# First attention batch in tiles of 6, 6, 6 and 5 steps, its first tile scattered in two parts, and the last values moved around the last second mix

## The chip, the cores and the metric

The kernel runs on one core of one Trainium2 chip. The metric is device time in microseconds (us) of a whole execution; the kernel before has a median of 1279.26 us over three runs. Five engines appear below: PE (TensorE: matmuls into PSUM), DVE (VectorE), ACT (ScalarE), POOL (GpSimd) and SP (SyncE, which here only issues transfers). Transfers issued by SP or ACT run on the core's 16 DMA engines.

## What is computed

Attention with two mixes over the heads (4 batches, 12 heads, 448 rows, 64 columns), then two feed-forward layers over the 1792 tokens:

```python
scores = scale * np.matmul(q, k.transpose(0, 1, 3, 2))
scores = np.einsum('bhij,hg->bgij', scores, w_pre)       # first mix, over heads
scores = scores - np.max(scores, axis=-1, keepdims=True)
attn = np.exp(scores)
attn = attn / (np.sum(attn, axis=-1, keepdims=True) + 1e-09)
attn = np.einsum('bhij,hg->bgij', attn, w_post)          # second mix, over heads
x = np.matmul(attn, v)                                   # (B, H, S, D) -> x (B*S, H*D)
...
gate = 1.0 / (1.0 + np.exp(-(x @ w_gate)))
x = gate * (x @ w_val) @ w_out                           # 768 -> 1536 -> 768
h = np.maximum(x @ w_in, 0.0)
return (h * h @ w_out2).astype(np.float32)               # 768 -> 2048 -> 768
```

## The kernel before

**Tiles and steps.** The rows of a batch are cut into tiles, and a tile into steps of 20 rows (`STEP`). A batch has 23 steps: 92 steps in all. `row_tiles` (L34) gives tiles of 6, 6, 6, 5 steps, but for batch 0 tiles of 3, 5, 5, 5, 5. So there are 17 tiles; tile 0 is steps 0 to 2, tile 1 steps 3 to 7, and batch 1 begins with step 23, batch 2 with step 46, batch 3 with step 69. The last tile of a batch has one step with half of its rows.

**What a tile needs.** `scores` (L192) makes the product of q and k for one tile and one of the 6 pairs of heads (eight matmul records), copies it from PSUM into a buffer `e` (rows on partitions), and scatters `e` with two transfers, one for each head, into `g`, where heads and rows lie on partitions as the first mix needs them. There are two `g`, used by even and odd tiles in turn, and six buffers `e`. A tile thus costs 12 scatters (210 KB each with 120 rows). The scores of a tile are spread over the first steps of the tile before (`plan`, L336 to 346). In the very beginning ("early", L376 to 383) the six pairs of tile 0 and four pairs of tile 1 are made first; there the two heads' PSUM banks are copied by ACT and by DVE, and of most pairs the second head's scatter is issued by ACT.

**What a step needs.** `premix` (L220, matmul line L226) is the first mix from `g`; DVE takes the maximum (L242), ACT the exponential (L250), DVE the reciprocal of the sum (L258, L259), POOL the scaled weights `wn` (L262), PE the second mix (`postmix`, L278), and DVE copies its PSUM into the buffer of mixed rows `ap` (`mixed`, L294). Step s issues the second mix of step s-3, the first mix of step s, and the scores or values planned for s, each engine strictly in the written order.

**Values.** When a tile's mixed rows are complete, `values` (L296, matmul line L313) multiplies them with v: three calls for each tile, 40 matmul records each, followed by DVE copies (L331). They are planned 3, 4 and 5 steps into the next tile. For the last tile but one they stand at steps 91, 92 and 93, for the last tile at 94, where also the last second mix (of step 91) is issued.

**SP.** One list of transfers in fixed order: q of a tile (`q_load`), k and v of a batch (224 KB and 320 KB for a pair of heads), the scatters, and for the feed-forward part `raw` (weights from HBM, 384 KB), `gv` (converted weights back to HBM, three of 384 KB and one of 192 KB for each conversion) and `w`. Once `sp.open` is set, a scatter waits until the sixth transfer before it in the list has landed, any other until the third before it (`Window`, L514).

**The feed-forward part** is placed by a planner (`Feed`): each step of attention gives it some modelled time, in which it hands out conversions and operand work to idle places of DVE, ACT, POOL and SP. From the end of the values on, PE does 4290 matmuls (L953) back to back.

Of the kernel before, what the change touches and what calls it, by code (L numbers as in the profile page):

```python
# [9 lines left out]
F32 = mybir.dt.float32  # L10
# [10 lines left out]
GI = 10  # L21
STEP = 2 * GI
HB = GI // 2
# [10 lines left out]
def row_tiles(b, S):  # L34

    n = -(-S // STEP)
    lengths = [n // 4 + (t < n % 4) for t in range(4)]
    if b == 0:
        lengths = [3] + [(n - 3) // 4 + (t < (n - 3) % 4) for t in range(4)]
    cuts = [0]  # L40
    for x in lengths:
        cuts.append(min(cuts[-1] + x * STEP, S))
    return list(zip(cuts, cuts[1:], lengths))
# [4 lines left out]
    return (length * STEP - (i1 - i0)) // GI * GI  # L48


def row_order(i0, i1, length):

    c, lead = length * GI, skipped(i0, i1, length)
    rows = []
    for y in range(2):
        for r in range(HB):
            for g in range(2 * length):  # L60
                rows.append(min(max(y * c + g * HB + r - lead, 0), i1 - i0 - 1) + i0)
    return rows


def attention(tc, feed, q, k, v, w_pre, w_post, B, H, S, D):
# [10 lines left out]
    nc = tc.nc  # L76
    sp = feed.sp
    NP = H // 2
    JB = S // HP
# [5 lines left out]
    tiles, steps, starts = [], [], []  # L85
    for b in range(B):
        for i0, i1, length in row_tiles(b, S):
            lead = skipped(i0, i1, length)
# [4 lines left out]
    NT, NS = len(tiles), len(steps)  # L93
    starts.append(NS)
    sizes = [t[3] * STEP for t in tiles]
    IM = max(sizes)
# [7 lines left out]
    with ExitStack() as ctx, ExitStack() as mix, ExitStack() as low, ExitStack() as top, ExitStack() as left:  # L104
# [17 lines left out]
        wr = p0.tile([P, 2, H], F32, name="wr")  # L122
        mask = p0.tile([P, HB, H], F32, name="mask")
        first = ap[1][:HP, :HB, :H]
        g_of = [None, None]
        for m, x in zip(((NT - 1) % 2, NT % 2), pg):
            g_of[m] = x.tile([P, GT, S], F32, name=f"g{m}")
# [63 lines left out]

        def scores(n, p, ps, early=None):  # L192

            b, _, _, length, _ = tiles[n]
            isz = sizes[n]
            kt = k_t.pop((b, p)) if last_of(n) else k_t[b, p]
            for c in range(0, isz, HP):
                c1 = min(c + HP, isz)
                for o in range(2):
                    r = slice(o * D, (o + 1) * D)  # L200
                    nc.tensor.matmul(  # L201
                        ps[c:c1, o, :S] if early is None else ps[o][c:c1, :S], lhsT=q_t[n][r, p, c:c1], rhs=kt[r], start=True, stop=True
                    )
            e = p4.tile([IM, 2, S], F32, tag="e", name="e")
            if early is None:
                nc.scalar.copy(e[:isz], ps[:isz, :, :S])  # L206
            else:
                nc.scalar.copy(e[:isz, 0], ps[0][:isz, :S])
                nc.vector.tensor_copy(e[:isz, 1], ps[1][:isz, :S])
            to = g_of[n % 2][G0 : G0 + GI * H].rearrange("(r h) g j -> h r g j", h=H)  # L210
            for o in range(2):
                x = dict(out=to[2 * p + o, :, : 2 * length], in_=e[:isz, o])
                if o and early:
                    nc.scalar.dma_start(**x)
                else:
                    sp.dma_start(**x, depth=2 * DEPTH)

        a_t = {}

        def premix(s):  # L220
            n, t, ys = steps[s]
# [69 lines left out]

        def mixed(n, t, ps):
            to = mixed_of(n)[:, :, t * GI : (t + 1) * GI].rearrange("p x (u i) -> p u x i", i=HB)
            nc.vector.tensor_copy(to, ps[:, :, : JB * KH].rearrange("p u (x i) -> p u x i", i=HB))  # L294

        def values(n, i):  # L296

# [49 lines left out]
        for n in range(NT):  # L347
            s0 = starts[n + 1] + LAG
            if n + 1 < NT:
                at = [s0, s0 + 1, s0 + 2]  # L350
                if n + 2 == NT:
                    at = [NS - 1, NS, NS + 1]
            else:
                at = [s0 - 1] * 3
            for i in range(NP // VP):
                plan[at[i]].append(("values", n, i))

        loads = {s: [] for s in range(NS + 12)}
        for i in range(NP):
            loads[i // 2].append((v_load, 0, i))  # L360
        firsts = [n for n in range(1, NT) if tiles[n][0] != tiles[n - 1][0]]
        for n in firsts:
            b = tiles[n][0]
# [8 lines left out]
            k_load(0, p)  # L372
            k_load(0, p + 1)
        masks()
        q_load(1)
        early = [(0, p) for p in range(NP)] + [(1, p) for p in range(fetched[1])]  # L376
        with tc.tile_pool(name="ps_s", bufs=1, space=PSUM, **kw) as ps_s:
            ps = [ps_s.tile([P, BANK], F32, name=f"ps_s{m}") for m in range(8)]
            for m, (n, p) in enumerate(early):
                x = 2 * m % 8  # L380
                scores(n, p, ps[x : x + 2], m % 4 != 3)
                if m == NP - 1:
                    mixers()
        ps_t = ctx.enter_context(tc.tile_pool(name="ps_t", bufs=1, space=PSUM, reuse_waits="tile", **kw))
        ps_m = mix.enter_context(tc.tile_pool(name="ps_m", bufs=1, space=PSUM, reuse_waits="tile", side="left"))
        pair_m = [ps_m.tile([P, 2, BANK], F32, name=f"ps_m{m}") for m in range(2)]
        pair_x, pair_y = (ps_t.tile([P, 2, BANK], F32, name=f"pair_{m}") for m in "xy")
        q_load(2)
        sp.open = True

        for s in range(NS + LAG):
# [46 lines left out]
            if 9 <= s < NS:  # L438
                n, t, _ = steps[s]
                if t < quiet[n]:  # L440
                    feed.free["SP"] = feed.now + 3.3
                feed.step(3.3)
            elif s >= NS:
                feed.step(3.0)


# [847 lines left out]
```

## Time and profile before

| what | before |
|---|---|
| median of 3 runs (lowest to highest) | 1279.26 us (1277.84 to 1281.04) |
| profiled execution | 1274.76 us, its span 1273.0 us |
| PE busy | 1221.9 us (96%) |
| PE weight loads busy | 1029.4 us (81%) |
| DVE busy | 909.2 us (71%) |
| ACT busy | 722.9 us (57%) |
| POOL busy | 300.0 us (24%) |
| chain that ended last, by engine | PE 89%, DVE 4%, DMA 3%, ACT 2%, issue 2% |

The span begins at the first instruction of the trace. Attention takes the first 383 us of it, the feed-forward layers the other 890 us. PE is the engine nearly everywhere, so what counts is where PE waits or runs at the lower of its two clocks.

### The profile page before, as it was taken

The page shows a single profiled execution, that of the slowest core. Times are in us where ns is not written, and L with a number is a line of the kernel's source. Part 1 is how long each engine was busy: PE and PEld are TensorE (multiplying, and loading weights), DVE is VectorE, ACT ScalarE, POOL GpSimd, SP SyncE. Part 2 cuts the span into 40 slices and gives each one's busy share as a digit, 9 for nine tenths or more (in the row PEclk, how much of TensorE's full clock was granted, in tenths as well). Part 3 has the DMA queues.
Part 4 walks back from the last instruction along what each step waited for, and adds up shares of the span by engine and source line. Part 5 has one row for each costly group of instructions (what it writes and reads, how often), then busy time and mean ns, then how long its engine had stood idle before and what let it go on. Part 6 is the DMA issues. An engine that isn't in the chain of part 4 may idle for free.

```text
span 1273.0 us, 31908 instructions
## 1 busy us (share of the span) xinstructions
PE 1221.9 (96%) x12882; PEld 1029.4 (81%) x12882; DVE 909.2 (71%) x1498; ACT 722.9 (57%) x1317; POOL 300.0 (24%) x381
## 2 busy tenths in 40 slices
PE   6999899989979999999999999999999999999998
PEld 2566566656658999899999999998889999999997
DVE  3667576757776567776657898577998788887621
ACT  4666667556645566576566538545566556336610
POOL 4223232314354323314232001123223220000000
PEclk9999999999979999999999999999999999999999
DMA  6666767675616987778996322757787875441231
GB/s 206 192 221 192 238 192 240 199 234 183 223 42 227 316 283 269 257 233 276 304 296 236 116 62 81 237 179 250 257 308 227 288 247 161 119 124 51 66 111 53
DMA packets 118927, 254.54 MB, mean 200 GB/s; under 512 B 12476, under 2 KB 65276, under 8 KB 118780
## 3 DMA queue, kind: packets, MB, share of 16 engines
q1 hardware_dynamic: 117840, 251.42, 60.6%
q8 instruction: 101, 1.65, 0.5%
q10 hardware_dynamic: 940, 1.09, 0.3%
q14 instruction: 46, 0.38, 0.1%
HBM read 153.71 MB, written 59.18 MB: 167 GB/s over the span
## 4 chain that ended last, share of the span: by engine, by line
PE 89%; DVE 4%; DMA 3%; ACT 2%; issue 2%; SPq 0%; POOL 0%; DVEq 0%; ACTq 0%; POOLq 0%
PE ps L953 67%; PE pair_y L313 6%; PE ps_m L226 5%; PE pair_x L278 4%; PE ps_m L201 3%; PE pair_y L201 2%; DMA g<-e 2%; DVE c L969 1%; ACT e L206 1%; DVE c L940 1%; ACT a L250 1%; PE ps_s L201 1%; DVE w L927 1%; DMA v<-in_v 0%; SPq L515 0%
## 5 line engine op out<-in xcount | busy, mean ns | idle before, releaser
L953 PE MATMUL ps<-c,w 128*128 128x448 f32 x4290 | 879.6, 367 | 6.4 <-ACT w L924 2.0
L953 PEld LDWEIGHTS ps<-c,w 128*128 128x128 f32 x4290 | 807.0, 188 | 78.8 <-ACT ps L977 2.5
L927 DVE TENSOR_TENSOR w<-w,w 128x768 fp32r<-128x768 f32 x189 | 198.7, 1052 | 149.4 <-ACT w L924 148.7
L829 POOL TENSOR_TENSOR y<-y,raw 128x384 int32<-128x384 int32 x136 | 157.7, 1182 | 470.3 <-DVE y L823 167.2
L924 ACT CAST w<-w 128x768 fp32r<-128x768 f32 x189 | 157.5, 835 | 161.0 <-PE ps L953 140.7
L937 ACT CAST c<-c 128x448 fp32r<-128x448 f32 x250 | 127.7, 565 | 70.0 <-DVE c L969 65.8
L940 DVE TENSOR_TENSOR c<-c 128x448 fp32r<-128x448 f32 x248 | 151.9, 661 | 9.6 <-ACT c L937 6.4
L969 DVE TENSOR_TENSOR c<-ps,c 128x448 f32<-128x448 f32 x172 | 105.7, 621 | 74.2 <-PE ps L953 68.5
L250 ACT ACTIVATE a<-ps_m,nm 128x448 f32<-128x448 f32 x180 | 112.8, 635 | 55.4 <-DVE nm L242 50.6
L262 POOL TENSOR_SCALAR wn<-wq,sm 128x60 f32<-128x60 f32 x180 | 75.5, 435 | 248.2 <-DVE sm L259 170.0
L242 DVE TENSOR_REDUCE nm<-ps_m 128x2 f32<-128x896 f32 (+1 forms) x92 | 98.2, 1069 | 47.0 <-PE ps_m L226 45.7
L278 PEld LDWEIGHTS pair_x<-wn,a 64*64 64x64 f32 x5040 | 91.7, 137 | 40.9 <-issue 21.5
L313 PEld LDWEIGHTS pair_y<-ap,v 128*64 128x64 f32 x2040 | 85.5, 142 | 34.9 <-issue 21.4
L294 DVE COPY ap<-pair_x 128x840 f32<-128x840 f32 x92 | 94.6, 1029 | 22.8 <-PE pair_x L278 21.5
L226 PE MATMUL ps_m<-g,wp 64*64 64x448 f32 (+1 forms) x720 | 91.3, 559 | 16.1 <-DMA g<-e 7.9
L278 PE MATMUL pair_x<-wn,a 64*64 64x60 f32 x5040 | 97.8, 222 | 8.4 <-POOL wn L262 5.9
L977 ACT COPY c<-ps 128x448 f32<-128x448 f32 x128 | 67.3, 533 | 62.8 <-PE ps L953 60.6
L313 PE MATMUL pair_y<-ap,v 128*64 128x60 f32 (+4 forms) x2040 | 96.5, 251 | 5.8 <-DVE ap L294 3.2
L969 DVE TENSOR_TENSOR c<-c 128x448 f32<-128x448 f32 x160 | 97.1, 641 | 1.8
L206 ACT COPY e<-ps_m 120x896 f32<-120x896 f32 (+1 forms) x46 | 41.6, 905 | 51.1 <-PE ps_m L201 50.5
L817 ACT ACTIVATE raw<-raw 128x768 f32<-128x768 f32 x68 | 62.3, 917 | 0.0
L820 ACT ACTIVATE raw<-raw 128x768 int32<-128x768 uint32 x68 | 62.3, 916 | 0.0
(49 smaller groups left out, 602.2 us busy)
## 6 DMA issues: line engine op xcount, KB each, us to landing
w<-gv SPq DMA_DIRECT2D x84, 384.0 KB
g<-e SPq DMA_DIRECT2D x108, 210.0 KB
raw<-in_wo SPq DMA_DIRECT2D x56, 384.0 KB
w<-wi SPq DMA_DIRECT2D x56, 384.0 KB
w<-wo SPq DMA_DIRECT2D x49, 384.0 KB
wo<-y SPq DMA_DIRECT2D x42, 384.0 KB
g<-e SPq DMA_DIRECT2D x81, 175.0 KB
gv<-y SPq DMA_DIRECT2D x36, 384.0 KB
```

The costliest lines, as they stand in the source:

```text
L226: nc.tensor.matmul(ps[u * HP : (u + 1) * HP, y, :S], lhsT=wp[r], rhs=g_of[n % 2][r, 2 * t + u], start=True, stop=True,)
L242: nc.vector.tensor_reduce(out=nm[:, ys], in_=a_t[s][0][:, ys, :S], op=ALU.max, axis=AX.X, negate=True)
L250: nc.scalar.activation(a[:, y], ps[:, y, :S], AF.Exp, bias=nm[:, y : y + 1], accum_out=sm[:, y : y + 1])
L278: nc.tensor.matmul(out[c : c + HP, u, 2 * k + (y if j < JB - 1 else 0)], lhsT=a[r, y, j * HP : (j + 1) * HP], rhs=wn[r, y].rearrange("p g ...
L313: nc.tensor.matmul(ps[o * D : (o + 1) * D, lo : lo + to], lhsT=w[:, o, j], rhs=rhs, start=j == 0, stop=j == JT - 2, skip_group_check=j >= ...
L829: e.tensor_tensor(out=y3, in0=y3, in1=of(raw.tile.bitcast(I32)[:, :, 0])[:, i], op=ALU.add)
L924: e.copy(dst.tile[:, 0], flat())
L927: e.tensor_tensor(out=dst.tile[:, 1], in0=flat(), in1=dst.tile[:, 0].bitcast(F32), op=ALU.subtract)
L937: e.copy(hi.tile, src.tile)
L940: e.tensor_tensor(out=lo.tile, in0=src.tile, in1=hi.tile.bitcast(F32), op=ALU.subtract)
L953: e.matmul(bank.tile, lhsT=a[k], rhs=x[l], start=start and n == 0, stop=stop and n == 2, skip_group_check=more,)
L969: e.tensor_tensor(out=out.tile, in0=a.tile, in1=b.tile, op=op)
```

## The change

- Batch 0 is cut like the others: tiles of 6, 6, 6, 5 steps; 16 tiles instead of 17, with the same 92 steps. Tile 0 is now steps 0 to 5, tile 1 steps 6 to 11.
- Tile 0's 120 rows are laid out so that partitions 0 to 59 of its score buffer hold what steps 0 to 2 need, and 60 to 119 what steps 3 to 5 need (`parts_of`, and `row_order` on the host). Its 12 scatters become 24 of half the size: first the first halves of all pairs, then, behind the last pair, the second halves of all pairs in reverse order, all of these on SP.
- Tile 0's score buffers are no longer the six `e` but pieces of the buffers of mixed rows (`spare`), five of `ap1` and one of `ap0`, which are not yet used then.
- In the beginning, q of tile 1 is loaded after the scatters of the second pair instead of ahead of all scatters; tile 1's scatters are all issued by SP; q of tile 2 and v of batch 0 are issued at steps 0 and 3 onwards instead of ahead of and at step 0 (in the list q of tile 3 stands ahead of q of tile 2).
- At the end, the values of the last tile but one move from steps 91, 92, 93 to 92, 93, 94, so that their third call stands behind the last second mix. The copy of that last second mix is split between DVE and ACT, and for the step before it the planner keeps DVE and ACT free of feed-forward work for 3 us of its modelled time.

```diff
     lengths = [n // 4 + (t < n % 4) for t in range(4)]
-    if b == 0:
-        lengths = [3] + [(n - 3) // 4 + (t < (n - 3) % 4) for t in range(4)]
...
+def parts_of(b, i0, length):
+
+    if b == 0 and i0 == 0:
+        return [(0, length), (length, 2 * length)]
+    return [(0, 2 * length)]
...
-    for y in range(2):
-        for r in range(HB):
-            for g in range(2 * length):
-                rows.append(min(max(y * c + g * HB + r - lead, 0), i1 - i0 - 1) + i0)
+    for g0, g1 in parts:
+        for y in range(2):
+            for r in range(HB):
+                for g in range(g0, g1):
+                    rows.append(min(max(y * c + g * HB + r - lead, 0), i1 - i0 - 1) + i0)
...
+        spare = []
+        for x in ap[::-1]:
+            x = x.rearrange("p x c -> p (x c)")[:, HB * (IM // 2) :]
+            x = x[:, : x.shape[1] // (2 * S) * 2 * S].rearrange("p (n o s) -> p n o s", o=2, s=S)
+            spare += [x[:, n] for n in range(x.shape[1])]
...
-            e = p4.tile([IM, 2, S], F32, tag="e", name="e")
+            if n == 0:
+                e = spare[p][:IM]
+            else:
+                e = p4.tile([IM, 2, S], F32, tag="e", name="e")
...
-            for o in range(2):
-                x = dict(out=to[2 * p + o, :, : 2 * length], in_=e[:isz, o])
-                if o and early:
-                    nc.scalar.dma_start(**x)
+            for m, (g0, g1) in enumerate(parts_of(b, i0, length)):
+
+                def scatter(m=m, g0=g0, g1=g1):
+                    for o in range(2):
+                        x = dict(out=to[2 * p + o, :, g0:g1], in_=e[g0 * GI : g1 * GI, o])
+                        if o and early and not m:
+                            nc.scalar.dma_start(**x)
+                        else:
+                            sp.dma_start(**x, depth=2 * DEPTH)
+
+                if m:
+                    late.append(scatter)
                 else:
-                    sp.dma_start(**x, depth=2 * DEPTH)
+                    scatter()
...
-            nc.vector.tensor_copy(to, ps[:, :, : JB * KH].rearrange("p u (x i) -> p u x i", i=HB))
+            x = ps[:, :, : JB * KH].rearrange("p u (x i) -> p u x i", i=HB)
+            if n == NT - 1 and t == tiles[n][3] - 1:
+                nc.vector.tensor_copy(to[:, 0], x[:, 0])
+                nc.scalar.copy(to[:, 1], x[:, 1])
+            else:
+                nc.vector.tensor_copy(to, x)
...
-                    at = [NS - 1, NS, NS + 1]
+                    at = [NS, NS + 1, NS + 2]
...
-            loads[i // 2].append((v_load, 0, i))
+            loads[3 + i // 2].append((v_load, 0, i))
...
-        q_load(1)
...
-                scores(n, p, ps[x : x + 2], m % 4 != 3)
+                scores(n, p, ps[x : x + 2], n == 0 and m != 3)
+                if m == 1:
+                    q_load(1)
                 if m == NP - 1:
                     mixers()
+                    for x in late[::-1]:
+                        x()
+        loads[0].append((q_load, 2))
...
-        q_load(2)
...
+                if s == NS + 1:
+                    for e in ("ACT", "DVE"):
+                        feed.free[e] = max(feed.free[e], feed.now + 3.0)
                 feed.step(3.0)
```

**SP in the beginning.** First what SP issues from its start up to step 3 or so in the kernel before, then in the changed one (`g_189` and `g_190` are the two `g`, `e` and `ap_...` the score buffers they are filled from):

```order
L515 DMA q<-in_q 128x600
L515 DMA g_189<-e 10x6x448 x7
L515 DMA g_190<-e 10x10x448 x5
L515 DMA q<-in_q 128x600
L515 DMA g_190<-e 10x10x448 x4
L515 DMA q<-in_q 128x600
L515 DMA v<-in_v 128x640 x6
```

```order
L548 DMA g_190<-ap_186 10x6x448 x2
L548 DMA q<-in_q 128x720
L548 DMA g_190<-ap_186 10x6x448 x4
L548 DMA g_190<-ap_185 10x6x448 x3
L548 DMA g_190<-ap_186 10x6x448 x10
L548 DMA g_189<-e 10x12x448 x12
L548 DMA q<-in_q 128x600
L548 DMA q<-in_q 128x720
L548 DMA v<-in_v 128x640 x6
```

Tile 0's scatters on SP grow from 7 to 19, tile 1's from 9 to 12, and the q that step 6's scores read now stands behind all of them.

**SP around the beginning of batch 2.** The scatters of the last tile of batch 1 (10 groups of 10 rows, `10x10x448`), then what stands between them and the scatters of the first tile of batch 2; before, then after:

```order
L515 DMA g_189<-e 10x10x448 x12
L515 DMA q<-in_q 128x720
L515 DMA k<-in_k 128x448 x3
L515 DMA raw<-in_wg 128x768
L515 DMA g_190<-e 10x12x448 x12
```

```order
L548 DMA g_189<-e 10x10x448 x12
L548 DMA q<-in_q 128x720
L548 DMA k<-in_k 128x448
L548 DMA raw<-in_wg 128x768 x2
L548 DMA k<-in_k 128x448
L548 DMA raw<-in_wg 128x768 x2
L548 DMA k<-in_k 128x448
L548 DMA gv_139<-y 128x384
L548 DMA g_190<-e 10x12x448 x12
```

Three loads of weights and one store have moved ahead of these scatters; in the kernel before, the same list (with `in_wv`) stands one batch later, ahead of the scatters of step 69.

**PE at the end of attention.** From the first mix of the last step on, second mixes (`pair_x`), values of the last tile but one (`64x120` and `64x60`) and the beginning of the last tile's values (`64x100`); before, then after:

```order
L226 MATMUL ps_m_327<-g_189,wp 64x448 x4
L313 MATMUL pair_y<-ap_186,v 64x120 x2
...
L278 MATMUL pair_x<-wn,a 64x60 x28
...
L278 MATMUL pair_x<-wn,a 64x60 x28
...
L313 MATMUL pair_y<-ap_186,v 64x120 x4
L278 MATMUL pair_x<-wn,a 64x60 x28
L313 MATMUL pair_y<-ap_185,v 64x100 x2
```

```order
L248 MATMUL ps_m_345<-g_189,wp 64x448 x4
L300 MATMUL pair_x<-wn,a 64x60 x28
...
L300 MATMUL pair_x<-wn,a 64x60 x28
...
L300 MATMUL pair_x<-wn,a 64x60 x28
L340 MATMUL pair_y<-ap_185,v 64x120 x2
...
L340 MATMUL pair_y<-ap_185,v 64x120 x4
L340 MATMUL pair_y<-ap_186,v 64x100 x2
```

The call of values that stood ahead of the first of these three second mixes now stands behind the last one, ahead of the last tile's values.

## Rows read from the trace of the kernel before

**Rows 1.** Windows: stretch, length, busy us (instructions) by engine, clock, DMA share, GB/s

```profile
18.59:41.33 22.74, 16.73 (x321) 8.04 (x321) 11.00 (x20) 12.63 (x28) 3.66 (x9) 0.85 0.72 231
41.33:106.01 64.68, 61.68 (x1649) 39.16 (x1649) 45.58 (x93) 42.04 (x93) 18.28 (x39) 1.00 0.62 198
106.01:359.27 253.26, 233.72 (x6137) 155.74 (x6140) 184.27 (x364) 158.35 (x353) 79.51 (x155) 0.98 0.65 207
359.27:382.88 23.61, 18.42 (x431) 15.63 (x422) 15.07 (x27) 10.17 (x21) 12.26 (x14) 0.78 0.19 53
382.88:1273.00 890.12, 879.65 (x4292) 807.00 (x4290) 646.60 (x983) 492.40 (x812) 174.95 (x148) 1.00 0.61 201
```

**Rows 2.** Timeline of 0 to 45 us: start, us, engine, line, instructions [idle before <-releaser]

```profile
6.96 13.67 SPq L515 DMA_DIRECT2D g<-e  x12
20.72 0.45 SPq L515 DMA_DIRECT2D q<-in_q  x1
26.22 0.97 PE L201 MATMUL pair_y<-k,q 64*64 64x448 f32 x8 [1.70 <-DMA q<-in_q]
29.48 1.77 PE L226 MATMUL ps_m<-g,wp 64*64 64x448 f32 x8 [2.29 <-DMA g<-e]
34.66 10.10 SPq L515 DMA_DIRECT2D g<-e  x12
```

**Rows 3.** Instructions on tile g, 0 to 50 us: count, ns min/median/max

```profile
L515 SPq DMA_DIRECT2D g<-e x29: 748/756/1714, 7.0 to 49.4; - x29
```

**Rows 4.** Chain that ended last, in order of time: start us, us, what

```profile
45.35 1.31 PE pair_y L313 x40
...
49.40 0.75 PE ps_m L201 x8
...
63.65 1.65 PE pair_y L313 x40
...
339.76 1.87 PE pair_y L313 x40
```

**Rows 5.** Windows of the first mix's line alone (PE busy, instructions), clock, DMA

```profile
175.55:193.48 17.93, 4.98 (x36) 1.00 0.65 207
215.92:258.59 42.67, 11.48 (x96) 1.00 0.67 210
```

**Rows 6.** Windows right behind three waits for scatters, columns as in rows 1

```profile
29.48:34.74 5.26, 5.26 (x77) 2.86 (x81) 1.78 (x4) 1.89 (x4) 0.84 (x2) 0.50 0.96 306
153.49:160.00 6.51, 6.51 (x117) 3.98 (x120) 3.07 (x5) 3.07 (x7) 0.84 (x2) 0.74 0.77 251
279.90:288.00 8.10, 8.10 (x136) 5.01 (x140) 3.13 (x7) 3.85 (x7) 0.84 (x2) 0.79 0.78 274
```

**Rows 7.** PE's waits, 50 to 400 us: us in total, times, longest

```profile
PE ps_m L226 <- DMA g<-e: 5.7, 2, 2.9
```

**Rows 8.** SP's timeline, 100 to 300 us: start, us, line, transfers

```profile
129.81 1.25 SPq L515 DMA_DIRECT2D gv<-y  x2
...
197.90 11.99 SPq L515 DMA_DIRECT2D g<-e  x12
```

**Rows 9.** Timeline of the end of attention, 360 to 385 us, columns as in rows 2

```profile
360.84 2.85 PE L313 MATMUL pair_y<-ap,v 128*64 128x120 f32 x40
361.35 0.84 POOL L262 TENSOR_SCALAR wn<-wq,sm 128x60 f32<-128x60 f32 x2 [0.40 <-DVE sm L259]
370.27 1.10 PE L278 MATMUL pair_x<-wn,a 64*64 64x60 f32 x56 [0.94 <-POOL wn L262]
371.71 1.90 DVE L927 TENSOR_TENSOR w<-w,w 128x768 fp32r<-128x768 f32 x1
374.61 3.12 PE L313 MATMUL pair_y<-ap,v 128*64 128x100 f32 x40 [3.23 <-DVE ap L294]
378.24 2.49 PE L313 MATMUL pair_y<-ap,v 128*64 128x100 f32 x40 [0.51 <-DVE x L331]
381.24 1.72 PE L313 MATMUL pair_y<-ap,v 128*64 128x100 f32 x40 [0.51 <-DVE x L331]
```

More of the change, by code (lines that the diff above doesn't have):

```diff
@@ L48, in skipped, with row_order @@
     return (length * STEP - (i1 - i0)) // GI * GI
-def row_order(i0, i1, length):
+def parts_of(b, i0, length):
+    if b == 0 and i0 == 0:
+        return [(0, length), (length, 2 * length)]
+    return [(0, 2 * length)]
+def row_order(i0, i1, length, parts):
     c, lead = length * GI, skipped(i0, i1, length)
     rows = []
-    for y in range(2):
-        for r in range(HB):
-            for g in range(2 * length):
-                rows.append(min(max(y * c + g * HB + r - lead, 0), i1 - i0 - 1) + i0)
+    for g0, g1 in parts:
[3 more added lines that the diff above has]
+                    rows.append(min(max(y * c + g * HB + r - lead, 0), i1 - i0 - 1) + i0)
     return rows
@@ L192, in scores @@
         def scores(n, p, ps, early=None):
-            b, _, _, length, _ = tiles[n]
+            b, i0, _, length, _ = tiles[n]
             isz = sizes[n]
@@ L210, in scores @@
             to = g_of[n % 2][G0 : G0 + GI * H].rearrange("(r h) g j -> h r g j", h=H)
-            for o in range(2):
-                x = dict(out=to[2 * p + o, :, : 2 * length], in_=e[:isz, o])
-                if o and early:
-                    nc.scalar.dma_start(**x)
-                else:
-                    sp.dma_start(**x, depth=2 * DEPTH)
-        a_t = {}
+            for m, (g0, g1) in enumerate(parts_of(b, i0, length)):
[8 more added lines that the diff above has]
+                    late.append(scatter)
+                else:
+                    scatter()
+        late, a_t = [], {}
         def premix(s):
@@ L1268 @@
         "q": np.concatenate(
-            [qt[b][:, :, row_order(*t)].ravel() for b in range(B) for t in row_tiles(b, S)]
+            [qt[b][:, :, row_order(*t, parts_of(b, t[0], t[2]))].ravel() for b in range(B) for t in row_tiles(b, S)]
         ),
```

## The prediction

> **What bounds the kernel now.** I read the windows first [rows 1]. From 382.88 us on PE is busy 879.65 of 890.12 us at full clock; nothing in the change touches that part but the planner's order, so the change is worth what it moves the end of attention. In attention PE waits in three places. From 18.59 to 41.33 us it is busy 16.73 of 22.74 us at a granted clock of 0.85, between its two levels of 1.2 and 2.4 GHz: the beginning is bound by transfers. From 41.33 to 359.27 us it is busy 295.4 of 317.9 us: PE itself is the bound, with single gaps. From 359.27 to 382.88 us it is busy 18.42 of 23.61 us at clock 0.78: the end is bound by what DVE does between PE's pieces.
>
> Then the places. In the timeline of the beginning [rows 2] PE waits 1.70 us at 26.22 for a q and 2.29 us at 29.48 for tile 1's scatters; step 6 has its first mix at 41.33. The list of waits [rows 7] has only two waits for scatters later, 5.7 us together, at steps 35 and 69. The windows behind such waits show what comes on top: clock 0.50, 0.74 and 0.79 for 5.26, 6.51 and 8.10 us [rows 6], that is 2.6, 1.7 and 1.7 us of lost time. At the end [rows 9] the last tile's values wait 3.23 us for the copy of the last second mix, which stands on DVE behind a feed-forward subtraction of 1.90 us, and then run at the lower level: 3.12 and 2.49 us for what takes 1.65 at full clock [rows 4].
>
> All sums are made against the profiled execution, 1274.76 us. It lies 4.5 us under the median of 1279.26; I carry the difference over.
>
> **The beginning, up to step 6.** Removed: the wait for tile 1 at step 3, since steps 3 to 5 now belong to tile 0. Its place is taken by two later dates on SP's list. An issue of a scatter takes SP 0.756 us [rows 3], with 105 KB as with 175 KB. Today the twelve scatters from 6.96 us on take 13.67 us [rows 2] with their waits for copies. The first seven and one q should be out at about 13.8 us (6.96 + 7 x 0.756 + 0.45 for the q + 1.1 for waits; an estimate). The q of tile 0 is twice as large, 360 instead of 180 KB, some 0.8 us at the 231 GB/s of rows 1, spread over three loads, of which the first alone delays PE's start. The twelve second halves follow: 12 x 0.756 = 9.1 us, out at 22.9, landed two to five us later. Step 3 can be had there at about 26 instead of 29.48. Then tile 1's twelve scatters of 210 KB, 10.1 to 12.0 us [rows 2, 8]: out at 33.0 to 34.9. Behind them stand two q's of 0.45 us each, tile 3's ahead of the one that step 6 reads. Today's q was issued at 20.72 and landed at 26.2 [rows 2], 5.5 us; so the date is about 39.5. PE needs scores of 0.97 us ahead of the first mix, at the lower clock nearer to 1.5: step 6 at 41.0 instead of 41.33. The buffers `spare` take away the waits for an `e` in the early scores, but those are hidden by the same dates.
>
> The scores of the tile that is saved, 6 x 0.75 = 4.5 us of PE [rows 4], are the ones of these first 41 us, when PE has time. What remains at step 6 is the same in both: 14 tiles' scores. But PE now comes out of an idle stretch of some five us, where today it has done so at 29.48 and has the slow part behind it. I charge the 2.6 us of rows 6 again: in effect 43.6 instead of 41.33.
>
> **Steps 6 to 22.** Values cost three pieces for each tile: 1.31 us each with 3 steps, 1.65 with 5, 1.87 with 6 [rows 4]. Those in these steps sum to 3.93 + 4.95 + 4.95 + 3.30 = 17.1 us now, and 5.61 + 5.61 + 3.74 = 15.0 after: 2.1 us less. So 64.68 us [rows 1] become 62.5. Twelve steps of later batches took 42.67 and a last tile of five 17.93 us [rows 5], 60.6 for the same 17 steps; between the two I take 61.4. Step 23 then comes at 105.0 instead of 106.01: **-1.0 us**, with bounds of -5 (step 6 at 38, no slow part) and +2 (step 6 at 42.5, 62.5 us behind it).
>
> **The transfers of batches 1 to 3.** The planner issues conversions earlier now, and SP's list is in order. What stands ahead of the scatters for step 46 is word for word (with another weight) what stood ahead of those for step 69: 12 x 210 + 360 + 3 x 224 + 4 x 384 + 192 = 5280 KB in a five-step period. There PE waited half of the 5.7 us of rows 7 and lost 1.7 us by the clock, 4.5 together. So +4.5 at step 46, where today 3936 KB cause no wait for scatters. At step 69 the list shrinks to 4704 KB (three whole stores instead of four loads and a small store); by interpolation 2.5 us of the 4.5 stay: -2.0. For step 81, two pairs of weight loads now lie among the v: 2520 + 300 + 4 x 384 + 1920 + 192 = 6468 KB, exactly the sum for step 35 today, which costs 4.5 us; but there SP also stood until the store at 129.81 us [rows 8] had its converted weights, and that wait isn't among these. I take a third, +1.5. Step 35 itself gets one small store less ahead of its values: -0.5. Together **+3.5 us**; bounds 0 (the extra loads fit in) and +7 (steps 35, 46 and 81 at the full price, 69 at 2.5).
>
> **The end of attention.** The values call that stood ahead of the first of the three last second mixes (360.84 us, 2.85 us long) covered the time until that mix's weights were there (361.35 + 0.84). PE will wait there, 1.3 us. In return it works 1.87 us behind the last second mix, while DVE and ACT each copy one half; both are free, since the planner keeps feed-forward work away and the 1.90 us subtraction goes behind the values. Gone: 3.23 us and most of the 0.94 us [rows 9]. Added: 1.3 us, and one wait of 0.51 us for the copies out of `pair_y`, of which there are two now. That is 2.36 us. If PE is back at full clock, the last values save 1.47 + 0.84 us more: 4.7. Sparse work ahead of 359 us is as it was, and the first of the moved calls may still run slow, so I take **-3.6 us**, bounds -4.7 and -1.5. What follows has its operands as today: 1.0 us of subtraction is pushed behind the values, but its weights are first needed by the 22nd matmul, 4.3 us later at 0.205 us each (879.65 us through 4290). I cost that, and the planner's other order in the feed-forward part, at nothing, +-2.
>
> Sum: -1.0 + 3.5 - 3.6 = -1.1 us. 1274.76 becomes 1273.7; on the scale of the median 1278.2.
>
> **A rule beside the trace.** SP's issue took 0.756 us for 105 KB and for 175 KB alike [rows 3], so cutting a transfer in two costs SP twice. The Trainium skill, DMA: Bandwidth & Descriptors, section Rules for kernel authors, says to coalesce many small transfers into a large one, and that under 64 KB one pays mostly overhead. By that rule the direction is against this change, yet a half of 105 KB would still pay for its bytes: 1260 KB at 231 GB/s are 5.5 us instead of the 9.1 us of issue in my sum, which would give -4.7 instead of -1.1.
>
> **The rivals.**
> *The lists cost nothing.* The second halves flow at the rate of their bytes, 3.6 us sooner, and the conversions that moved find room (DMA share 0.65 in rows 1), so no new wait arises: -1.0 - 3.6 + 0 - 4.7 = -9.3, 1270.0. For it: the DMA engines are never full in these windows. Against it: the same list did cause a wait at step 69.
> *SP's list decides, slower than before.* Everything goes through one queue. If tile 1's scatters land slower than 1.0 us each, the q for step 6 comes at 42, three us later (+1.5 for the beginning), and the full +7 is paid at steps 35, 46 and 81: 1.5 + 7 - 3.6 = +4.9, 1284.2. It decides from the point where scatters for step 46 miss it by more than 3 us.
> *The end doesn't gain.* PE only moves its idle time from behind the last second mix to ahead of the first of the three, at low clock: -1.0 + 3.5 + 0 = +2.5, 1281.8.
>
> **How the numbers follow.** Forecast 0.46, the lists cost nothing 0.34, SP's list decides 0.13, the end doesn't gain 0.07. About 0.3%, 3.8 us, is what a measurement of this kernel can tell from no change. Faster by more: the second case and 0.04 of the forecast's, 0.38. Slower by more: the third and 0.04 of the others, 0.17. Within: 0.45. The range takes in the two outer cases but for the far ends of their bounds: 1268.5 to 1285. The forecast's own runs from 1273 to 1283.
>
> **What the profile after would show.** Right: no wait at step 3 or a short one, PE idle ahead of step 6 and waiting for a q near 39 us, then slow matmuls; the wait of 2.3 to 2.9 us for scatters at step 46 instead of 69; the last values right behind the last second mix, at full clock; the feed-forward part again 890 us. Wrong: step 6 well ahead of 40 us, no wait for scatters at 46 or 81, or a feed-forward part that is longer or shorter by more than 2 us, whose order I haven't priced.

## Result and profile after

The change makes the kernel slower: 1285.31 us median of the kernel after beside 1275.93 us of the kernel before, 20 executions each, run beside each other; ratio 1.0068, interval [1.0042, 1.0094]. The ratio is taken from the fast runs alone, without one run of the kernel after that was in a slower state, the medians from all. The forecast was no change (1278.2 beside 1279.26 us), and the time lies 0.3 us above its range of 1268.5 to 1285.

The profiled execution of after took 1288.81 us, its span 1287.0 us, against 1274.76 and 1273.0 us. The page has PE's work about as before and PE later. Its line of busy time, and its line on the chain that ended last by engine:

```profile
PE 1216.2 (94%) x12738; PEld 1023.5 (80%) x12738; DVE 903.9 (70%) x1491; ACT 718.8 (56%) x1312; POOL 297.2 (23%) x382
...
PE 84%; DMA 8%; DVE 4%; ACT 2%; issue 1%; SPq 1%; POOL 0%; ACTq 0%; DVEq 0%; POOLq 0%
```

The share of DMA in the chain has grown from 3% to 8%, about 65 us: the chain now goes through transfers where it went through PE. The windows of the same five parts as in [rows 1], columns as there (step 6 to step 23 is the second row, step 23 to step 91 the third):

```profile
22.80:44.10 21.30, 11.41 (x288) 5.42 (x284) 11.64 (x20) 9.03 (x26) 4.18 (x10) 0.85 0.66 214
44.10:107.00 62.90, 60.09 (x1524) 38.32 (x1520) 43.31 (x86) 40.56 (x88) 17.50 (x37) 0.97 0.66 207
107.00:378.90 271.90, 237.74 (x6140) 154.59 (x6135) 185.00 (x366) 162.10 (x358) 81.19 (x158) 0.96 0.60 192
378.90:398.94 20.04, 17.29 (x428) 14.59 (x424) 10.38 (x25) 7.15 (x18) 15.07 (x18) 0.82 0.16 43
398.94:1287.00 888.06, 875.69 (x4292) 805.90 (x4290) 646.62 (x983) 492.65 (x812) 167.89 (x143) 1.00 0.61 202
```

Step 23 begins at 107.0 instead of 106.0 us (+1.0). The third stretch takes 271.9 instead of 253.3 us (+18.6). The end takes 20.0 instead of 23.6 us (-3.6), the feed-forward part 888.1 instead of 890.1 us (-2.1). So all of the loss of this execution lies in batches 1 to 3. PE is busy 4.0 us longer there at a clock of 0.96 instead of 0.98, and idle 14.6 us longer. PE's timeline shows where; these are its waits of over 1.5 us for transfers in that stretch and, as the first row, the one ahead of step 6 (columns as in [rows 2]):

```profile
42.52 1.76 PE L212 MATMUL pair_y<-k,q 64*64 64x448 f32 x8 [6.78 <-DMA q<-in_q]
...
157.42 1.77 PE L248 MATMUL ps_m<-g,wp 64*64 64x448 f32 x8 [5.86 <-DMA q<-in_q]
...
202.88 1.77 PE L248 MATMUL ps_m<-g,wp 64*64 64x448 f32 x8 [5.71 <-DMA g<-e]
...
293.64 0.98 PE L248 MATMUL ps_m<-g,wp 64*64 64x448 f32 x8 [1.56 <-DMA g<-e]
...
342.34 1.77 PE L248 MATMUL ps_m<-g,wp 64*64 64x448 f32 x8 [4.78 <-DMA g<-e]
```

They are the first mixes of steps 35, 46, 69 and 81. Line 248 does not read q; at 157.42 the q is only the transfer issued right behind the last scatter, so I read this too as a wait for scatters. Windows right behind the four (as in [rows 6]):

```profile
157.42:163.93 6.51, 6.51 (x112) 3.02 (x116) 3.12 (x5) 2.94 (x6) 2.78 (x4) 0.75 0.55 173
202.88:210.98 8.10, 8.10 (x124) 4.94 (x128) 2.64 (x6) 3.00 (x7) 0.83 (x2) 0.66 0.75 266
293.64:301.74 8.10, 8.10 (x200) 5.10 (x204) 4.65 (x10) 4.27 (x8) 3.06 (x5) 1.00 0.42 136
342.34:350.44 8.10, 8.10 (x136) 4.33 (x140) 3.37 (x5) 4.15 (x8) 0.84 (x2) 0.63 0.51 177
```

With the lost time by the clock (length times one less the clock) the steps cost: 46, 5.71 + 2.75 = 8.5 us, nothing before; 81, 4.78 + 3.0, and 1.13 for a late v at 334.77, 8.9 us, nothing before; 35, 5.86 + 1.6 = 7.5 instead of 4.5 us; 69, 1.6 instead of 4.6 us. That is +17.4 of the 18.6 us. Behind 293.64 the clock stays at 1.00, so the wait of 1.56 us costs only itself.

### The profile page after: what moved, and what is told of

Read it like the earlier page. It is cut to its first block, busy times and chain, and to the rows that moved or that the text cites. A ratio compares the mean times of both kernels' runs of the same rounds, so it can differ in the third digit from the quotient of the medians.

```text
span 1287.0 us, 31568 instructions
## 1 busy us (share of the span) xinstructions
PE 1216.2 (94%) x12738; PEld 1023.5 (80%) x12738; DVE 903.9 (70%) x1491; ACT 718.8 (56%) x1312; POOL 297.2 (23%) x382
## 4 chain that ended last, share of the span: by engine, by line
PE 84%; DMA 8%; DVE 4%; ACT 2%; issue 1%; SPq 1%; POOL 0%; ACTq 0%; DVEq 0%; POOLq 0%
PE ps L986 66%; PE pair_y L340 5%; PE ps_m L248 4%; DMA g<-e 4%; PE pair_x L300 4%; PE ps_m L212 3%; PE pair_y L212 2%; DMA k<-in_k 1%; DMA q<-in_q 1%; DVE c L1002 1%; DVE c L973 1%; DMA v<-in_v 1%; ACT e L220 1%; PE ps_s L212 1%; DVE nm L264 1%
## 5 line engine op out<-in xcount | busy, mean ns | idle before, releaser
L340 PEld LDWEIGHTS pair_y<-ap,v 128*64 128x64 f32 x1920 | 81.4, 140 | 31.2 <-issue 15.5
L340 PE MATMUL pair_y<-ap,v 128*64 128x120 f32 (+3 forms) x1920 | 92.6, 252 | 5.8 <-DMA v<-in_v 1.9
L220 ACT COPY e<-ps_m 120x896 f32<-120x896 f32 (+1 forms) x43 | 38.9, 906 | 65.8 <-PE ps_m L212 63.7
L248 PEld LDWEIGHTS ps_m<-g,wp 64*64 64x64 f32 (+1 forms) x720 | 24.7, 137 | 49.4 <-issue 30.1
```

Source lines behind the costliest of these rows:

```text
L248: nc.tensor.matmul(ps[u * HP : (u + 1) * HP, y, :S], lhsT=wp[r], rhs=g_of[n % 2][r, 2 * t + u], start=True, stop=True,)
L340: nc.tensor.matmul(ps[o * D : (o + 1) * D, lo : lo + to], lhsT=w[:, o, j], rhs=rhs, start=j == 0, stop=j == JT - 2, skip_group_check=j >= ...
```

## Experiments

The first theory (A): SP's list in batches 1 to 3, where weight loads now stand ahead of the scatters for steps 46 and 81, is the whole loss. The rivals seek it in the beginning or behind attention. For the late step 6 the question is whether SP's dates decide it (A1) or what PE has done up to then. All ratios are to the kernel before, run on the same chip; one per cent is 12.8 us. A trace shows one execution of a kernel, the ratio comes from many.

**The list alone, both ways.** The planner's first step of modelled time, one number, decides the list, and with it when the conversions run on the other engines. With 10 the changed kernel gets, from batch 1 on, the list of the kernel before word for word; with 7 the kernel before gets that of the changed one from about step 41 on.

```diff
-            if 9 <= s < NS:
+            if 10 <= s < NS:
```

> The changed kernel with one number altered: the planner begins at step 10 instead of 9. From the second tile of batch 1 on, SP's list is then word for word that of the kernel before; tiles, beginning and end stay as changed. Theory A (the planner's conversions, moved ahead on SP's list, make the scatters late): PE's waits for scatters at steps 46 and 81 go, a smaller one comes back at step 69, the end of attention falls from 398.9 us to about 387, and the time is some 12 us below the changed kernel's, near the kernel before (ratio 0.995 to 1.002). Theory B (the new beginning shifts everything, and the list is innocent): still 1.005 or more.

Measured: 0.9952 [0.9925, 0.9980], 1.2% (some 15 us) under the changed kernel and faster than the kernel before. From step 23 to step 91 its trace has, in one window:

```profile
108.40:359.50 251.10, 231.63 (x6140) 153.00 (x6135) 184.33 (x365) 158.43 (x353) 79.44 (x156) 0.99 0.64 207
```

20.8 us less than after, with as many matmuls. The opposite edit in the kernel before:

```diff
-            if 9 <= s < NS:
+            if 7 <= s < NS:
```

> The kernel before with the planner beginning at step 7 instead of 9, which gives it the changed kernel's list of transfers from step 35 on (four weight loads and a small store ahead of the scatters of step 46, loads among the v ahead of step 81); tiles, beginning and end as before. Theory A: slower by 8 to 15 us, ratio 1.006 to 1.012, with waits for scatters at steps 46 and 81. Theory B: within 0.3%.

Measured: 1.0054 [1.0021, 1.0088]. That is a little less than expected. Step 46, without a wait in [rows 7], now has one, and nothing else of the change is in this kernel:

```profile
194.32 1.77 PE L226 MATMUL ps_m<-g,wp 64*64 64x448 f32 x8 [4.10 <-DMA g<-e]
...
314.17 0.81 PE L278 MATMUL pair_x<-wn,a 64*64 64x60 f32 x39 [2.18 <-issue]
```

The wait that was expected at step 81 isn't in this trace. PE had stood for 2.18 us before, in a second mix (second row) for which the profile names no transfer, then ran at a clock of 0.80 (310.79 to 318.15 us), and came to step 81 at 329.06 us without a wait. This execution, 1274.63 us, is also the fastest of its twelve and no slower than the profiled one of the kernel before, so here only the ratio shows the loss.

So the planner's start makes the loss, from either side: 15 +- 5 us and 7 +- 4 us. It moves the list and the conversions together; the experiments below that put single groups of loads back show that it is the loads. What stands in the list shows in SP's timeline ahead of the scatters for step 46. First the changed kernel (step 41 begins at 179.8 us), then the kernel with the list of before (step 41 at 177.7 us):

```profile
173.44 0.43 SPq L548 DMA_DIRECT2D q<-in_q  x1
174.71 0.33 SPq L548 DMA_DIRECT2D k<-in_k  x1
177.35 1.23 SPq L548 DMA_DIRECT2D raw<-in_wg  x2
179.41 0.33 SPq L548 DMA_DIRECT2D k<-in_k  x1
180.54 1.38 SPq L548 DMA_DIRECT2D raw<-in_wg  x2
182.40 0.33 SPq L548 DMA_DIRECT2D k<-in_k  x1
185.41 0.33 SPq L548 DMA_DIRECT2D gv<-y  x1
185.78 11.20 SPq L548 DMA_DIRECT2D g<-e  x12
```

```profile
171.86 0.42 SPq L548 DMA_DIRECT2D q<-in_q  x1
173.03 3.10 SPq L548 DMA_DIRECT2D k<-in_k  x3
177.34 0.33 SPq L548 DMA_DIRECT2D raw<-in_wg  x1
178.90 9.87 SPq L548 DMA_DIRECT2D g<-e  x12
```

The issues themselves are short. The list is late by the gaps between them, and it has 2.7 us of gap ahead of the one store (182.73 to 185.41). It is the longest of SP's waits for loads of these weights to land (100 to 380 us; us in total, times, longest):

```profile
SPq L548 <- DMA raw<-in_wg: 7.1, 6, 2.7
```

The converted weights that the store takes had been written by 179.20 us. The scatters begin 6.0 us after step 41 instead of 1.2 us, and their last lands when PE has waited 5.71 us.

**The end alone.** The kernel before with only the three edits of the end (values one step later, last copy on two engines, DVE and ACT kept free).

```diff
-            nc.vector.tensor_copy(to, ps[:, :, : JB * KH].rearrange("p u (x i) -> p u x i", i=HB))
+            x = ps[:, :, : JB * KH].rearrange("p u (x i) -> p u x i", i=HB)
+            if n == NT - 1 and t == tiles[n][3] - 1:
+                nc.vector.tensor_copy(to[:, 0], x[:, 0])
+                nc.scalar.copy(to[:, 1], x[:, 1])
+            else:
+                nc.vector.tensor_copy(to, x)
...
-                    at = [NS - 1, NS, NS + 1]
+                    at = [NS, NS + 1, NS + 2]
...
+                if s == NS + 1:
+                    for e in ("ACT", "DVE"):
+                        feed.free[e] = max(feed.free[e], feed.now + 3.0)
```

> The kernel before with only the end of the change: values of the last tile but one a step later, split copy of the last second mix, DVE and ACT kept free for one step. Both theories: from the last first mix to the first feed-forward matmul 20 us instead of 23.6 (in the changed kernel 20.0), so -3.6 us, ratio 0.997. If the end's gain hangs on something else in the change: 1.000.

Measured: 1.0008 [0.9976, 1.0040]. The trace has the gain, 19.0 us from step 91 to the feed-forward part instead of 23.6; the time doesn't show it. In this execution the feed-forward part is longer, 894.5 instead of 890.1 us. Taken by itself this is inconclusive; the two pairs below go on with it.

**The early q.** The changed kernel with q of tile 1 again ahead of all scatters.

```diff
+        q_load(1)
...
-                if m == 1:
-                    q_load(1)
```

> The changed kernel with tile 1's q loaded ahead of all scatters, as in the kernel before. The wait of 4.4 us for it at 15.3 us goes, and step 0 has its first mix at about 19 instead of 22.8 us. Theory A1 (SP's dates set step 6): step 6 stays at 43 to 44 us, time unchanged within 1.5 us. Theory B1 (the late q delays everything behind it): step 6 four us earlier, and the time 4 us less.

Measured: 1.0070 [1.0040, 1.0101]. PE reaches step 0 at 17.5 instead of 22.8 us, and step 6 at 44.2 instead of 44.1 us. So when step 0 begins doesn't matter for step 6, and SP's dates decide it: A1 holds.

**The list of before without the end.** The kernel with 10, with the three edits of the end undone.

```diff
-                    at = [NS, NS + 1, NS + 2]
+                    at = [NS - 1, NS, NS + 1]
...
-            if 9 <= s < NS:
+            if 10 <= s < NS:
```

> e1 (the changed kernel with the planner from step 10 on, list of before) without the end of the change: values of the last tile but one at steps 91 to 93, whole copy of the last second mix on DVE. What the end is worth, taken from the other side: from the last first mix to the first feed-forward matmul 23 to 24 us instead of 20.2. Theory (the end gains 3.5 us in any surrounding): 1270 to 1271, ratio to before 0.998, against 0.995 of e1. Rival (what the end gains is given back in the feed-forward part, as e3 with 1.001 may show): the same time as e1 within 1 us, with a feed-forward part some 3 us shorter than e1's.

Measured: 1.0014 [0.9977, 1.0050], against 0.9952 with the end: 0.6% +- 0.5%, some 8 us, where 3.5 was expected. This is also the beginning of the change alone: +0.1% +- 0.4%.

**Both q early.** The kernel with 10, with q of tile 1 ahead of the scatters and q of tile 2 ahead of the second halves.

```diff
+        q_load(1)
...
-                if m == 1:
-                    q_load(1)
...
+                    q_load(2)
...
-        loads[0].append((q_load, 2))
```

> e1 with tile 1's q ahead of all scatters and tile 2's q ahead of the second halves of tile 0's scatters. Theory A1 (step 6 waits for its q, 7.8 us in e1, behind 24 scatters): the wait at 43 us goes, step 6 then waits for tile 1's scatters instead, which land at about 38 to 39, so step 6 is at 39 to 40 instead of 44.9 and the time some 4 us under e1's. Rival (the scatters of tile 1 land as late as the q did): step 6 at 43 or later, time as e1 within 1.5 us.

Measured: 0.9964 [0.9930, 0.9998]. Step 6 is at 42.1 us, 2.8 us sooner than with the late q's (44.9), and waits for tile 1's scatters instead. It was expected at 39 to 40 us with a time 4 us shorter; the ratio is no lower than with the late q's (0.9952).

**Whole scatters.** The same, with tile 0 in 12 scatters of 210 KB instead of 24 of 105 KB.

```diff
-        return [(0, length), (length, 2 * length)]
+        return [(0, 2 * length)]
```

> e6 with tile 0 scattered in one part, 12 transfers of 210 KB instead of 24 of 105 KB. SP has 12 issues of 0.76 us less, but steps 0 to 2 need all of it. Theory (SP's issues set the dates of the beginning): step 0 later, at 19 to 21 instead of 17.5, tile 1's scatters out 5 to 6 us sooner, step 6 at 35 to 36; the time 2 to 4 us under e6's. Rival (bytes set the dates, not issues): step 6 as in e6 within 1 us, time as e6 or more.

Measured: 0.9946 [0.9908, 0.9984]. In SP's and PE's timeline the last scatter of tile 1 is out and the next q issued six us sooner, and step 6 follows without a wait:

```profile
18.35 11.63 SPq L547 DMA_DIRECT2D g<-e  x12
...
32.72 0.34 SPq L547 DMA_DIRECT2D q<-in_q  x1
...
37.91 0.95 PE L248 MATMUL ps_m<-g,wp 64*64 64x448 f32 x8
```

Step 0 comes later (22.8 instead of 17.4 us), step 6 4.2 us sooner than with halves (37.9 against 42.1; expected was 35 to 36). The split buys an early start that nothing uses.

**One group of loads put back at a time.** In the changed kernel the fifth conversion's weight loads, which lay between the v ahead of step 81, behind those scatters; and in another kernel the third conversion's, which lay ahead of step 46, from step 46 on, by which the last conversion's loads go behind the scatters of step 81 too (`x` is a task of the planner, 3.3 us its modelled time of a step).

```diff
+            if count[0] == 5 and x.on[0][0] == "SP":
+                x.ready = (82 - 9) * 3.3
```

> The changed kernel with one conversion held back: the four weight loads that stand among the v ahead of step 81 come behind all scatters; all else is the changed kernel's list. Theory A (each moved group costs at its own step): the wait for scatters at step 81 (4.8 us, then slow matmuls) goes, the waits at 35 and 46 stay; 6 to 8 us less than the changed kernel, ratio to before 1.000 to 1.002. Rival (the wait at 81 has another cause, the v's alone): the wait stays, ratio 1.007.

Measured: 1.0028 [0.9999, 1.0058], some 5 +- 5 us under the changed kernel. The wait at step 81 is gone; those at 35 (3.53 us) and 46 (4.19 us) stay.

```diff
+            if count[0] == 3 and x.on[0][0] == "SP":
+                x.ready = (46 - 9) * 3.3
```

> The changed kernel with one thing put back: the loads of the third conversion of weights may be issued by SP from step 46 on only. In SP's list they leave the place ahead of the scatters for step 46 (which has again one store and three loads of k, as cheap as in the kernel before) and now lie in pairs between the loads of v of batch 2, ahead of the scatters for step 58; the last conversion's loads, which lay like that ahead of step 81, go behind them as in the kernel before. If loads of weights between the v cost their full price wherever they stand, the wait at 46 goes (steps 41 to 52 take about 40 us instead of 48.6 us), the one at 81 goes (steps 75 to 87 about 42 us instead of 50.2 us), and a wait for scatters of 3 to 5 us stands at step 58, with matmuls at the lower clock behind it: ratio 0.998 to 1.002. If they cost a third of that, as the prediction took for step 81, nothing over 1.5 us stands at step 58 and the ratio is that of the kernel with the list of before, 0.995.

Measured: 1.0003 [0.9969, 1.0037]. The waits at 46 and 81 are gone, the one at 35 stays (4.58 us), and one stands where the loads now lie between the v, at step 58. PE at step 58, and the window behind it:

```profile
243.27 1.77 PE L248 MATMUL ps_m<-g,wp 64*64 64x448 f32 x8 [5.02 <-DMA k<-in_k]
...
243.27:251.37 8.10, 8.10 (x156) 4.51 (x160) 3.94 (x7) 4.47 (x8) 2.79 (x4) 0.70 0.50 149
```

(k at 243.27 is once more only the next transfer.) Loads of weights between the v cost 5.0 + 2.4 us there, not a third of it. With one reserve: step 58 had a wait of 4.1 us in the kernel with both q early and about 2 us in two others, without such loads.

**Whole scatters without the end.** The kernel with whole scatters, the edits of the end undone as above.

```diff
-                    at = [NS, NS + 1, NS + 2]
+                    at = [NS - 1, NS, NS + 1]
```

> The kernel with whole scatters for tile 0, both q ahead of them and the list of before, with its end put back to that of the kernel before (values of the last tile but one at steps 91, 92 and 93, the last copy on DVE alone, no time kept free). SP's list is word for word the same. If the end is worth its 3.6 us in the time, the end of attention takes 23 instead of 20 us in the trace and the ratio is 0.0028 higher than that of the kernel with the end, which had 0.9946: about 0.9974. If the end's gain is given back in the feed-forward part, as the time of the kernel before with the end alone (1.0008) would have it, the ratio is again 0.995 and the feed-forward part is shorter by as much as the end of attention is longer.

Measured: 0.9926 [0.9891, 0.9962], with a list that is word for word the same as with the end (0.9946) up to 380 us and has another order behind that, in the feed-forward part. It has the lowest ratio of all, 0.7% under the kernel before. The beginning of the last tile's values in this kernel, then in the one with the end:

```profile
363.92 3.12 PE L335 MATMUL pair_y<-ap,v 128*64 128x100 f32 x40 [3.29 <-DVE ap L316]
```

```profile
368.49 1.72 PE L340 MATMUL pair_y<-ap,v 128*64 128x100 f32 x40 [0.67 <-DVE x L358]
```

The end itself is 24.7 us without the edits and 19.9 us with them. But the feed-forward part is 886.6 us without and 894.5 us with them. A part of that is the edits' own. PE's first waits in the feed-forward part, without and then with the end:

```profile
378.66 4.39 PE L977 MATMUL ps<-c,w 128*128 128x448 f32 x20 [0.78 <-ACT ps L1001]
383.50 9.60 PE L977 MATMUL ps<-c,w 128*128 128x448 f32 x46 [0.45 <-DVE w L951]
393.71 6.55 PE L977 MATMUL ps<-c,w 128*128 128x448 f32 x31 [0.61 <-ACT ps L1001]
```

```profile
380.22 4.39 PE L985 MATMUL ps<-c,w 128*128 128x448 f32 x20 [1.11 <-ACT ps L1009]
385.37 9.61 PE L985 MATMUL ps<-c,w 128*128 128x448 f32 x46 [0.76 <-DVE w L959]
396.21 4.12 PE L985 MATMUL ps<-c,w 128*128 128x448 f32 x19 [1.24 <-ACT ps L1009]
```

With the end, these three waits sum to 3.1 instead of 1.8 us: 1.3 us are given back, at the 22nd matmul for the first time. The other 6 us or so are not waits: in the feed-forward part PE is idle 11.0 us without and 11.6 us with the end, and busy 875.6 and 883.0 us. The last section has them.

From step to step, in us, what each list costs (start of the first mix of the one step to that of the other, from each trace):

```
                              41-52  52-64  64-75  75-87  23-91
list of before
  before                       40.4   42.7   45.6   42.0  253.3
  after, list of before        40.3   42.3   44.5   42.1  251.1
  before, end alone            40.3   46.1   48.4   43.6  259.8
  list of before, no end       40.5   42.4   45.6   42.8  257.0
  both q early                 39.5   48.1   43.3   40.7  254.1
  whole scatters               40.1   43.5   47.2   41.2  256.0
  whole scatters, no end       38.8   43.4   42.9   41.0  248.0
list of after
  after                        48.7   44.4   42.7   50.2  271.9
  before, list of after        46.2   44.3   40.9   46.0  257.7
  after, early q               45.7   42.4   42.1   48.7  262.9
in part
  81 put back                  46.9   42.4   43.2   42.0  258.0
  46 put back                  39.5   48.7   41.6   41.0  256.9
```

The first column splits by the list alone: 40.0 us on average with that of before, 46.9 us where the loads stand ahead of step 46. So does the fourth: 41.9 against 48.3 us. The third goes the other way, 45.4 against 42.2 us.

## Why the prediction was wrong

**The transfers of batches 1 to 3: the step that failed.** The term of +3.5 us was too small. Its places and signs were right for three steps: a new wait at 46, one at 81, a smaller one at 69. The sizes were not. At step 46 it took +4.5 us from the waits of a single execution (2.75 and 2.90 us); the four traces with these loads have +6.9 us. At step 69 it took -2.0; they have -3.1. At step 81 it took a third of the price, +1.5, with the reason that at step 35 SP also stood until the store at 129.81 us had its converted weights. The trace of before doesn't bear that out. The last piece of them was written 12.6 us ahead of that store (first row), and the 2.2 us for which SP stood ahead of it are its longest wait for a load of weights to land (second row, 100 to 380 us as above):

```profile
116.67 0.56 DVE L851 TENSOR_TENSOR y<-y 128x384 f32<-128x384 f32 x1
...
SPq L515 <- DMA raw<-in_wv: 6.5, 5, 2.2
```

So this row gives no ground for a discount. The three traces with loads ahead of step 81 have +6.4 us: two of them with the wait there (4.78 and 3.80 us) and +7.6, the kernel before with the list of after with the stop at 314.17 us in its place. With the loads put back the wait is gone, and as far as one trace tells they cost as much at step 58. At step 35, where -0.5 was predicted, after's +3 us can be chance: kernels with its list waited 3.53 to 5.86 us there, those with the list of before 2.65 to 5.15 us. Together the columns give some +9.5 us where the sum had +3.5 (its bound +7); after's own profiled execution shows +18.6, since its waits of 5.71, 5.86 and 4.78 us are the longest of their steps. In the times, the two experiments on the list give +15 +- 5 and +7 +- 4 us.

The estimate by kilobytes in a five-step period named the right places, but it knows no gaps: the list in order is late by the sum of the gaps in which SP waits for an earlier transfer to land, 2.7 us of them ahead of one store at 185.41 us. And a wait that PE comes to costs its clock in addition: 2.75 and 3.0 us behind the new waits, more than the 1.7 us of [rows 6].

**The beginning: -1.0 predicted, +1.0 in the trace.** SP's and PE's timeline of after:

```profile
10.29 15.26 SPq L548 DMA_DIRECT2D g<-ap  x17
...
15.29 5.89 PE L212 MATMUL ps_s<-k,q 64*64 64x448 f32 x32 [4.37 <-DMA q<-in_q]
...
25.66 10.16 SPq L548 DMA_DIRECT2D g<-e  x12
...
38.02 1.24 SPq L548 DMA_DIRECT2D q<-in_q  x2
```

The second halves were out at 25.6 us, not at 22.9: with their waits the issues took 0.9 us each (17 in 15.26 us), where the sum had 0.756 and 1.1 us of waits in all. The late q of tile 1, for which PE waits 4.37 us, delays step 0; it isn't the cause here, since with that q early the halves were out at 24.9 us and step 6 came no sooner. Tile 1's scatters then took 10.2 us, as in [rows 2]. Then SP stood still for 2.2 us (35.82 to 38.02): as the kernel is written, a q waits until the third transfer before it has landed, and the prediction had both q's follow at once. So q for step 6 was there at 42.5 us and step 6 at 44.1 us, near the 43.6 us "in effect" of the prediction. Steps 6 to 22 took 62.9 us, where 61.4 plus the slow part, 64.0, was the sum. In the times the beginning is +0.1% +- 0.4%, no more than predicted.

SP's 19 issues of halves took 0.748 us each in the median, as the smallest in [rows 3]. By the Trainium skill, DMA: Bandwidth & Descriptors, section Rules for kernel authors, many small transfers belong in a large one; the two kernels that differ in this alone agree in the direction, with step 6 4.2 us sooner for the whole scatters, though their times (0.9946 and 0.9964) can't tell them apart. What the prediction drew from the same rule, second halves 3.6 us sooner at the rate of their bytes, didn't come.

**The end: right in the trace, -3.6 us.** The timeline of after, around the last second mix (389.30) and the last values:

```profile
381.78 1.76 PE L300 MATMUL pair_x<-wn,a 64*64 64x60 f32 x56 [1.07 <-POOL wn L284]
...
389.30 1.04 PE L300 MATMUL pair_x<-wn,a 64*64 64x60 f32 x56
390.27 1.92 PE L340 MATMUL pair_y<-ap,v 128*64 128x120 f32 x40
390.40 0.60 DVE L318 COPY ap<-pair_x 128x420 f32<-128x420 f32 x1 [0.52 <-PE pair_x L300]
391.04 0.56 ACT L319 COPY ap<-pair_x 128x420 f32<-128x420 f32 x1 [4.56 <-DVE ap L318]
...
392.85 1.72 PE L340 MATMUL pair_y<-ap,v 128*64 128x100 f32 x40 [0.67 <-DVE x L358]
```

The wait of 3.23 us of [rows 9] is gone, and the last values take 1.72 us instead of 3.12; the new wait ahead of the first of the three second mixes is 1.07 us, where 1.3 was predicted. The halves of the copy run one after the other (390.40 and 391.04), not side by side, which nobody waits for. What the prediction costed at nothing is not nothing everywhere: behind the list of before, the subtraction that moved behind the values makes the feed-forward part's first weights late by 1.3 us. In the times, three pairs with and without the end (the ratios of the second come from two chips, and so do those of the third) give +0.1% +- 0.3%, -0.6% +- 0.5% and +0.2% +- 0.5%, together -1 +- 3 us: neither the 3.6 us nor zero is excluded.

**The feed-forward part: 0 +- 2 predicted, -2.1.** At the edge of its bound in this execution; from 886.5 to 894.5 us in the others.

**The sum and the rival.** The working gave -1.1; with the terms as the traces of all kernels have them it is 1.0 + 9.5 - 3.6 - 2.1 = +4.8, and with those of after's own trace +14. The ratio gives +8.7 +- 3.3 us, between the two. "SP's list decides, slower than before" at 0.13 named what happened, by its own mechanism (step 6 at a q of 42, waits at 35, 46 and 81), and its +4.9 us is close to the former sum. The forecast at 0.46 rested on a price for step 46 from the waits of one execution and on a third of it for step 81, for which no row stood. That the time came out only 0.3 us above the range doesn't make the term right: +3.5 us stood where the columns have +9.5.

## What to carry to other kernels

Where one queue issues everything in order, an edit at one place that makes a planner start earlier is an edit of the whole list: compare that list step by step, and price each load that moves ahead of a transfer somebody waits for with the full wait plus the slow stretch behind it, and look in SP's own waits for what an issue stood for before discounting it. One execution is a thin ground for such a price: at step 69, where that of before shows 2.90 us, five others with its list show 2.35 to 4.07 us and a sixth no wait for scatters. A gain at the start of a stretch is worth something only if the date that ends the stretch moves with it; here an early step 0 (17.5 or 22.8 us) changed nothing about step 6, while fewer issues on SP did. And a gain that a trace shows at one place has to be looked for again in what follows, since the moved work can give part of it back.

## What the hardware showed beside

The kernels with whole scatters, with the end and without, do the same 4290 feed-forward matmuls and differ by 8 us there. A window of 100 us late in the feed-forward part, with the end and then without:

```profile
974.58:1074.58 100.00, 100.00 (x485) 90.83 (x484) 79.22 (x121) 58.63 (x97) 18.41 (x15) 1.00 0.70 230
```

```profile
973.35:1073.35 100.00, 100.00 (x495) 92.67 (x494) 81.46 (x125) 56.68 (x95) 18.52 (x15) 1.00 0.69 229
```

PE is busy all the time at a granted clock of 1.00 in both, and does 485 matmuls in 100 us in the one and 495 in the other, 2% slower; the next 100 us have the same two numbers, which makes some 4 us. The kernel before with the end alone shows the 485 too, the changed kernel with its end the 495. And the kernel with the list of before, which has the end and whose transfers behind attention come in the same order as those of the kernel with whole scatters and the end, does 495 there, with a feed-forward part of 887.7 instead of 894.5 us. So it is neither the end nor the list. What it is stays open. With it, and with waits for scatters at one step of one list that lie between 2.65 and 5.15 us (step 35, list of before), single executions of one kernel spread over 1.5% (1267.54 to 1286.38 us for the kernel before), so a profiled execution tells where the time goes, and only many runs how much.
